# One decode step of grouped-query attention on one core: a tour of branches for TensorE, VectorE's heads as a loop, and the query loaded ahead of the first barriers

## The chip, the cores and the metric

The kernel runs on one core of a Trainium2 chip. The metric is the device time of one execution in microseconds, the median of three runs. The profile is that of one further execution, taken by the hardware profiler.

## The reference

One new token with 32 query heads attends to 65536 keys and values of 8 key/value heads, each of width 128, all in bfloat16. Each key/value head serves four query heads.

```python
B, Hq, Hkv, Sq, Sk, D = 1, 32, 8, 1, 65536, 128
scale = D ** -0.5
scores = jnp.einsum("bhqd,bhkd->bhqk", q, k) * scale   # k, v repeated for 4 query heads
p = _softmax(scores, axis=-1)
return jnp.einsum("bhqk,bhkd->bhqd", p, v)
```

K and V are 134 MB each. Each element is read once.

## The kernel before

The 8 key/value heads are taken one after the other (g = 0 to 7). The keys of a head lie in HBM as 128 partitions x 512 rows of 128 elements; one load (`load`, L116, issued by SyncE) brings half of them, 8 MB, as 128 rows of 64 KB. There are three buffers of that size: `bufA` and `bufB` take the two halves of K, `bufC` the two halves of V, one at a time. The last V goes elsewhere, as nothing more is to come: its first half to `bufA`, its second to `bufB` in seven pieces of `PIECES` rows, each with a semaphore of its own (`sP[0]` to `sP[6]`).

Each engine has its program written out by hand, with semaphores between them. The order of the loads is that of SyncE's queue (L132 to L155), each after the wait that says its buffer is free.

- VectorE (L199 to L258) first makes selector matrices out of an identity, and turns the query. Then, for each head, written out eight times: it turns each buffer of K in place, in two halves (`turn`, L221); takes the maximum of the scores (`mx`, L232); scales the result of the head before (`o_out`, L237); reduces the maxima further (`m4`, `mrow`, `nmb`); turns the exponentials (`E`, L254); takes the reciprocal of the sum (`rl`).
- TensorE (L298 to L438) makes the scores with `scores` (L316, 32 matmuls of 512 columns for each half buffer), the maxima with `maxima`, the sum with `sums`, and the product with V with `stream` (L333: four rows of V in one matmul of 512 columns, on one quarter of the array's columns, into `psum_o`). `pick` (L341) adds the diagonal blocks of `psum_o` by a selector into `psum_f`. Head 0's scores stand ahead of a loop of seven turns (L367), each with V of head g-1 and the scores of head g. Behind the loop comes the last V: `stream` on bufA; `idle(8)`, 16 matmuls whose results nobody reads; `stream` on the first piece; `idle(8)`; `stream` on the second piece; `pick`; then `quads` (L386, one row of V in a matmul of 128 columns, into `psum_s`) for the third and fourth pieces; `singles` (L395, straight into `psum_f`) for the last three; and one matmul (L433) that adds `s_sb`, the copy of `psum_s`.
- ScalarE copies `psum_o` to `o_sb`, makes the exponentials (L281), and at the end copies `psum_s` to `s_sb` (L289), scales the last head (L292) and stores it.
- GpSimd builds the constants, and for each head the stationary operand `wq` from the query (L183).

Ahead of all this stands the first load of `bufA`, issued between two barriers of all engines; everything else, the load of the query by ScalarE's queue (L261) too, is behind the second one.

Of the kernel before, what the change touches and what calls it, by code (L numbers as in the profile page):

```python
# [6 lines left out]

ALU = mybir.AluOpType
ACT = mybir.ActivationFunctionType
AX = mybir.AxisListType  # L10

G = 8
H = 4
P = 128
# [4 lines left out]
SLIDE = P + 4 * (W - 1)  # L19
PIECES = (128, 72, 28, 16, 4, 4, 4)  # L20


@with_exitstack
def kernel(
# [5 lines left out]
    out: bass.AP,  # L30
):


# [58 lines left out]
    kt = sem("kt")  # L92
    kdone = sem("kdone")
    vdone = sem("vdone")
# [4 lines left out]
    nms = sem("nms")  # L99
    qps = sem("qps")  # L100
    exd = sem("exd")
    ets = sem("ets")
    ocp = sem("ocp")
    outs = sem("outs")
    dl = sem("dl")
    pl = sem("pl")
    cleared = list(sems)
    sS = sem("sS")
# [13 lines left out]

    first = load(bufA, kr[0], 0)
    tc.no_tile_sem_insts.add(first.ins.name)
    first.then_inc(sA, 16)
    tc.add_to_no_dep_group("first", first.ins)
    tc.declare_fence(pool.nop().ins, group="first")
    tc.close()
    tc.compile()
# [4 lines left out]
    for g in range(1, G):  # L134
        sp.wait_ge(kdone, 2 * g - 1)
        load(bufA, kr[g], 0).then_inc(sA, 16)
        if g == 1:
            sp.wait_ge(kdone, 2)
            load(bufB, kr[1], 1).then_inc(sB, 16)
            sp.wait_ge(vdone, 1)  # L140
            load(bufC, vr[0], 1).then_inc(sC, 16)
            continue
        sp.wait_ge(vdone, 2 * (g - 1))
        load(bufC, vr[g - 1], 0).then_inc(sC, 16)
        sp.wait_ge(kdone, 2 * g)
        load(bufB, kr[g], 1).then_inc(sB, 16)
        sp.wait_ge(vdone, 2 * (g - 1) + 1)
        load(bufC, vr[g - 1], 1).then_inc(sC, 16)
    sp.wait_ge(kdone, 2 * G - 1)
    load(bufA, vr[G - 1], 0).then_inc(sA, 16)  # L150
    sp.wait_ge(kdone, 2 * G)
    at = 0
# [25 lines left out]
    for g in range(G):  # L178
        if g == 0:
            pool.wait_ge(exd, 1)  # L180
        else:
            pool.wait_ge(kdone, 2 * g)
        pool.tensor_tensor(  # L183
            out=wv[:, :, :, 0:H],
            in0=qv[:, :, g * H:(g + 1) * H].unsqueeze(2).broadcast_to([P, 4, 4, H]),
            in1=quad[:, :].unsqueeze(1).unsqueeze(3).broadcast_to([P, 4, 4, H]),
            op=ALU.mult,
        ).then_inc(wqs, 1)


    n_dl = [0]

    def after(ins):

        ins.then_inc(dl, 1)
        n_dl[0] += 1
        dve.wait_ge(dl, n_dl[0])

    dve.wait_ge(cst, 1)  # L199
    dve.tensor_reduce(  # L200
        out=quad[:, :], in_=ident[:, :].rearrange("p (a x) -> p a x", a=4), axis=AX.X, op=ALU.max
    )
    dve.tensor_reduce(
        out=selq[:, :], in_=ident[:, :].rearrange("p (j x) -> p x j", x=32), axis=AX.X, op=ALU.max
    )
    dve.tensor_reduce(
        out=sel[:, :], in_=ident[:, :].rearrange("p (x h) -> p h x", h=H), axis=AX.X, op=ALU.max
    )
    after(dve.tensor_reduce(
        out=s64[:, :], in_=ident[:, :].rearrange("p (j x) -> p x j", x=64), axis=AX.X, op=ALU.max  # L210
    ))
    dve.tensor_tensor(out=selx[:, :], in0=s64[:, 0:16], in1=s64[:, 48:64], op=ALU.add).then_inc(cst, 1)
# [9 lines left out]

    n_pes = 0
    for g in range(G):
        dve.wait_ge(sA, 16 * (g + 1))
        turn(bufA, 0)
        turn(bufA, 1)
        dve.wait_ge(sB, 16 * (g + 1))
        turn(bufB, 0)
        turn(bufB, 1)  # L230
        dve.wait_ge(kdone, 2 * (g + 1))
        dve.tensor_reduce(out=mx[:, :], in_=sc[:, :], axis=AX.X, op=ALU.max).then_inc(mxs, 1)  # L232
        if g > 0:

            n_pes += 1
            dve.wait_ge(pes, n_pes)
            dve.tensor_scalar_mul(  # L237
                out=o_out[:, (g - 1) * D:g * D], in0=psum_f[0:H, 0:D], scalar1=rl[:, 0:1]
            ).then_inc(outs, 1)
        n_pes += 1  # L240
        dve.wait_ge(pes, n_pes)
        after(dve.tensor_reduce(
            out=m4[:, :], in_=misc[0:1, 0:P].rearrange("o (x h) -> o h x", h=H), axis=AX.X, op=ALU.max
        ))
        dve.tensor_scalar_mul(
            out=mrow[:, :].rearrange("o (x h) -> o x h", h=H),
            in0=m4[:, :].unsqueeze(1).broadcast_to([1, 32, H]),
            scalar1=-SCALE,
        ).then_inc(mxs, 1)
        n_pes += 1  # L250
        dve.wait_ge(pes, n_pes)
        dve.tensor_copy(out=nmb[:, :], in_=misc[:, P:P + 1]).then_inc(nms, 1)  # L252
        dve.wait_ge(exd, g + 2)
        dve.transpose(out=E[:, 0:2048], in_=E[:, 0:2048]).then_inc(ets, 1)  # L254
        n_pes += 1
        dve.wait_ge(pes, n_pes)
        dve.reciprocal(out=rl[:, :], in_=misc[0:H, P + 4:P + 5]).then_inc(dl, 1)
        n_dl[0] += 1  # L258


    act.dma_start(out=qn[:, :], in_=q[0, :, 0, :]).then_inc(sQ, 16)  # L261
    act.wait_ge(qps, 1)
    act.copy(
        out=qx[:, :].rearrange("p (b r h) -> p b h r", b=2, r=2),
        in_=misc[:, 0:P].rearrange("p (b h r) -> p b h r", b=2, r=2),
    ).then_inc(exd, 1)

    def store(g, n):

        act.wait_ge(outs, g + n)  # L270
        act.dma_start(
            out=out[0, g * H:(g + n) * H, 0, :].rearrange("(g h) d -> h g d", h=H),
            in_=o_out[:, g * D:(g + n) * D].rearrange("h (g d) -> h g d", d=D),
        ).then_inc(sS, 16)

    for g in range(G):
# [7 lines left out]
        ).then_inc(exd, 1)  # L284
    store(0, G - 1)
    act.wait_ge(vdone, 2 * G)
    act.copy(out=o_sb[:, :], in_=psum_o[:, :]).then_inc(ocp, 1)  # L287
    act.wait_ge(vdone, 2 * G + 1)
    act.copy(out=s_sb[:, :], in_=psum_s[:, 0:D]).then_inc(ocp, 1)  # L289
    act.wait_ge(pes, n_pes + 1)  # L290
    act.wait_ge(dl, n_dl[0])
    act.activation(  # L292
        out=o_out[:, (G - 1) * D:G * D], in_=psum_f[0:H, 0:D], func=ACT.Copy, scale=rl[:, 0:1]
    ).then_inc(outs, 1)
    store(G - 1, 1)


    pe.wait_ge(cst, 4)  # L298
    pe.matmul(out=misc[:, 0:P], lhsT=rep[:, :], rhs=qt[:, :], start=True, stop=True).then_inc(qps, 1)  # L299

    def take(semaphore, n=1):

        pe.wait_ge(semaphore, n).then_inc(semaphore, -n)  # L303

    def scores(buf, x, s):

        take(kt)
        bank = sc[:, (2 * s + x) * 512:(2 * s + x + 1) * 512]
        T = buf[:, x * half // 2:(x + 1) * half // 2].rearrange(
            "p (c w b i r) -> p w b r c i", c=C, w=W, b=2, r=2  # L310
        )
        for w in range(W):
            for b in range(2):
                for r in range(2):
                    at = (2 * b + r) * SLIDE + 4 * (W - 1 - w)
                    last = pe.matmul(  # L316
                        out=bank, lhsT=wq[:, at:at + P], rhs=T[:, w, b, r],
                        start=(w + b + r == 0), stop=(w == W - 1 and b + r == 2),
                    )
        return last  # L320

# [4 lines left out]

    def stream(buf, s, lo, n, end):

        for row in range(lo, lo + n, 4):
            j = row // 4  # L330
            qd = slice(32 * (j % 4), 32 * (j % 4) + 32)
            at = column(s, row) // 32 * 32
            last = pe.matmul(  # L333
                out=psum_o[qd, :], lhsT=E[:, at:at + 32], rhs=buf[:, row * D:(row + 4) * D],
                start=(s == 0 and j < 4), stop=(s == 1 and row >= end - 16),
            )
        return last

# [8 lines left out]
    def maxima():  # L347
        take(mxs)
        pe.transpose(out=misc[0:1, 0:P], in_=mx[:, :], identity=ident[:, :]).then_inc(pes, 1)  # L349
        take(mxs)  # L350
        pe.matmul(  # L351
# [3 lines left out]
    def sums():  # L355
        take(ets)
        pe.matmul(  # L357
            out=misc[0:H, P + 4:P + 5], lhsT=sel[:, :], rhs=lsum[:, :], start=True, stop=True
        ).then_inc(pes, 1)

    take(wqs)
    scores(bufA, 0, 0)
    scores(bufA, 1, 0).then_inc(kdone, 1)
    scores(bufB, 0, 1)
    scores(bufB, 1, 1).then_inc(kdone, 1)
    maxima()
    with pe.Fori(1, G):  # L367
        sums()
        take(sC, 16)
        stream(bufC, 0, 0, NT, NT).then_inc(vdone, 1)  # L370
        take(wqs)
        scores(bufA, 0, 0)
        scores(bufA, 1, 0).then_inc(kdone, 1)
        scores(bufB, 0, 1)
        take(sC, 16)
        stream(bufC, 1, 0, NT, NT).then_inc(vdone, 1)
        scores(bufB, 1, 1).then_inc(kdone, 1)
        take(ocp)
        pick(True, True).then_inc(pes, 1)
        maxima()  # L380
# [28 lines left out]
    sums()  # L409
    pe.wait_ge(sA, 16 * (G + 1))  # L410
    stream(bufA, 0, 0, NT, NT).then_inc(vdone, 1)
    idle(8)
    at = 0
    for x in range(2):
        pe.wait_ge(sP[x], 16)
        last = stream(bufB, 1, at, PIECES[x], PIECES[0] + PIECES[1])
        at += PIECES[x]
        if x == 0:
            idle(8)
    last.then_inc(vdone, 1)  # L420
# [16 lines left out]
    pe.wait_ge(sP[6], 16)  # L437
    singles(at, PIECES[6], True).then_inc(pes, 1)  # L438

# [35 lines left out]
```

## Time and profile before

| | us |
|---|---|
| median of three runs (628.48 to 628.68) | 628.51 |
| the profiled execution | 628.52 |
| its span, first to last instruction | 626.6 |
| PE busy | 343.8 |
| DVE busy | 322.7 |
| ACT busy | 23.8 |
| POOL busy | 4.1 |
| HBM read | 268.44 MB |

In the views of the profile, PE is TensorE's matmuls, PEld its weight loads, DVE VectorE, ACT ScalarE, POOL GpSimd, SP SyncE. A row of the timeline gives the start, the duration, the engine, the line, the operation, the tiles written and read, the shape and the count; in brackets stands the engine's idle time before it and what ended it. A row of digits gives the busy share of equal slices in tenths. The program has two semaphore counts that matter below: `kdone`, which TensorE raises when it has used bufA and bufB of K, and for which SyncE, VectorE and GpSimd all wait; and `vdone`, the same for V.

### The profile page before, as it was taken

To read this page: it belongs to the slowest core of one execution; us is meant where nothing else is said; L and a number is where in the kernel's file an instruction comes from. 1 tells how busy PE (TensorE), PEld (TensorE's weight loads), DVE (VectorE), ACT (ScalarE), POOL (GpSimd) and SP (SyncE) were. 2 spreads that over 40 slices of the span, in tenths; PEclk is the share of its full clock that TensorE was granted. 3 is DMA by queue.
4 is the path that set the end of the run, shared out by engine and by line. 5 is a ranking of instruction groups with operands and counts; after the bars stand their busy time and mean duration, and the time that the engine had idled before them with its cause. 6 is when DMAs were issued, how large, how long until landed. Compare 5 with 4: busy or idle time off the path is not lost. (4 is left out here: it accounts for less than half of the span.)

```text
span 626.6 us, 4811 instructions
## 1 busy us (share of the span) xinstructions
PE 343.8 (55%) x2221; PEld 147.7 (24%) x2229; DVE 322.7 (52%) x93; ACT 23.8 (4%) x28; POOL 4.1 (1%) x19
## 2 busy tenths in 40 slices
PE   0097438850848408594094830948209592094957
PEld 0043213320323203231041310413104141041423
DVE  0587378539055490644906459073680826708230
ACT  1000100010000100001000010000100001000010
POOL 1000000000000000000000000000000000000000
PEclk9998679885798757787588975889658796597979
DMA  9999999999999999999999999999999999999997
GB/s 402 402 469 403 464 406 461 410 457 410 460 410 460 410 460 406 452 414 427 443 423 448 414 452 418 452 418 452 418 452 414 456 414 456 414 456 410 452 396 300
DMA packets 5565, 268.53 MB, mean 429 GB/s; under 512 B 696, under 2 KB 1080, under 8 KB 1336
## 3 DMA queue, kind: packets, MB, share of 16 engines
q1 hardware_dynamic: 5472, 268.44, 99.2%
q8 instruction: 4, 0.07, 0.0%
q10 hardware_dynamic: 88, 0.02, 0.0%
q14 instruction: 1, 0.01, 0.0%
HBM read 268.44 MB, written 0.01 MB: 428 GB/s over the span
## 5 line engine op out<-in xcount | busy, mean ns | idle before, releaser
L221 DVE STREAM_TRANSPOSE bufB<-bufB 128x8192 f32<-128x8192 f32 x16 | 138.4, 8690 | 130.5 <-DMA bufB<-in_k_dram 130.5
L316 PE MATMUL sc<-bufB,wq 128*128 128x512 bf16 x512 | 129.6, 415 | 55.8 <-PEq L303 55.8
L221 DVE STREAM_TRANSPOSE bufA<-bufA 128x8192 f32<-128x8192 f32 x16 | 138.2, 8673 | 15.5 <-DMA bufA<-in_k_dram 15.5
L333 PE MATMUL psum_o<-bufC,E 128*32 128x512 bf16 x896 | 66.2, 461 | 125.2 <-PEq L303 125.2
L316 PE MATMUL sc<-bufA,wq 128*128 128x512 bf16 x512 | 116.9, 387 | 27.7 <-PEq L303 27.7
L316 PEld LDWEIGHTS sc<-bufB,wq 128*128 128x128 bf16 x512 | 51.5, 103 | 133.4 <-issue 84.6
L316 PEld LDWEIGHTS sc<-bufA,wq 128*128 128x128 bf16 x512 | 49.2, 97 | 94.7 <-issue 37.1
L232 DVE TENSOR_REDUCE mx<-sc 128x1 f32<-128x2048 f32 x8 | 18.3, 2292 | 97.6 <-PE sc L316 97.6
L333 PEld LDWEIGHTS psum_o<-bufC,E 128*32 128x32 bf16 x896 | 29.8, 114 | 158.8 <-issue 146.8
L254 DVE STREAM_TRANSPOSE E<-E 128x2048 bf16<-128x2048 bf16 x8 | 18.5, 2312 | 17.0 <-ACT E L281 17.0
L357 PE MATMUL misc<-lsum,sel 128*4 128x1 f32 x16 | 1.5, 163 | 38.2 <-PEq L303 38.2
L279 ACT COPY o_sb<-psum_o 128x512 f32<-128x512 f32 x7 | 4.1, 585 | 437.1 <-PE psum_o L333 437.1
L281 ACT ACTIVATE E<-sc,nmb 128x2048 bf16<-128x2048 f32 x8 | 15.7, 1967 | 130.3 <-DVE nmb L252 130.3
L357 PEld LDWEIGHTS misc<-lsum,sel 128*4 128x4 f32 x16 | 0.9, 83 | 38.7 <-issue 38.7
L349 PE MATMUL misc<-ident,mx 128*1 128x128 f32 x8 | 2.3, 282 | 13.0 <-PEq L303 13.0
L341 PE MATMUL psum_f<-o_sb,selx 128*4 128x128 f32 x64 | 8.3, 273 | 0.7 <-ACT o_sb L287 0.7
L299 PE MATMUL misc<-qt,rep 32*128 32x128 bf16 x1 | 0.3, 284 | 13.2 <-DVE qt L214 13.2
L405 PE MATMUL sc<-bufA,wq 128*128 128x512 bf16 x24 | 6.7, 379 | 0.5 <-issue 0.2
L351 PE MATMUL misc<-one,mrow 1*128 1x1 f32 x16 | 3.4, 279 | 5.7 <-PEq L303 5.7
L341 PEld LDWEIGHTS psum_f<-o_sb,selx 128*4 128x4 f32 x64 | 4.9, 86 | 5.2 <-issue 3.0
L183 POOL TENSOR_TENSOR wq<-qx,quad 128x64 bf16<-128x64 bf16 x8 | 2.3, 292 | 512.9 <-PE sc L316 502.4
L333 PE MATMUL psum_o<-bufA,E 128*32 128x512 bf16 x64 | 5.3, 504 | 0.0
(41 smaller groups left out, 34.9 us busy)
## 6 DMA issues: line engine op xcount, KB each, us to landing
bufB<-in_v_dram SPq DMA_DIRECT2D x1, 4096.0 KB, 18.2
bufB<-in_v_dram SPq DMA_DIRECT2D x1, 2304.0 KB, 23.4
bufB<-in_v_dram SPq DMA_DIRECT2D x1, 896.0 KB, 25.1
bufB<-in_v_dram SPq DMA_DIRECT2D x1, 512.0 KB, 25.8
bufB<-in_v_dram SPq DMA_DIRECT2D x3, 128.0 KB, 25.5
bufC<-in_v_dram SPq DMA_DIRECT2D x14, 34.9
bufA<-in_k_dram SPq DMA_DIRECT2D x8, 37.4
bufB<-in_k_dram SPq DMA_DIRECT2D x8, 47.2
```

The lines of the kernel that those rows point to most:

```text
L183: pool.tensor_tensor(out=wv[:, :, :, 0:H], in0=qv[:, :, g * H:(g + 1) * H].unsqueeze(2).broadcast_to([P, 4, 4, H]), in1=quad[:, :].unsquee ...
L221: dve.transpose(out=kv, in_=kv).then_inc(kt, 1)
L232: dve.tensor_reduce(out=mx[:, :], in_=sc[:, :], axis=AX.X, op=ALU.max).then_inc(mxs, 1)
L254: dve.transpose(out=E[:, 0:2048], in_=E[:, 0:2048]).then_inc(ets, 1)
L279: act.copy(out=o_sb[:, :], in_=psum_o[:, :]).then_inc(ocp, 1)
L281: act.activation(out=E[:, 0:2048], in_=sc[:, :], func=ACT.Exp, bias=nmb[:, 0:1], scale=SCALE, accum_out=lsum[:, 0:1],).then_inc(exd, 1)
L316: last = pe.matmul(out=bank, lhsT=wq[:, at:at + P], rhs=T[:, w, b, r], start=(w + b + r == 0), stop=(w == W - 1 and b + r == 2),)
L333: last = pe.matmul(out=psum_o[qd, :], lhsT=E[:, at:at + 32], rhs=buf[:, row * D:(row + 4) * D], start=(s == 0 and j < 4), stop=(s == 1 and ...
L341: last = pe.matmul(out=psum_f[0:H, 0:D], lhsT=selx[:, H * x:H * x + H], rhs=o_sb[:, x * D:(x + 1) * D], start=(start and x == 0), stop=(st ...
L351: pe.matmul(out=misc[:, P:P + 1], lhsT=mrow[:, :], rhs=one[:, :], start=True, stop=True).then_inc(pes, 1)
L357: pe.matmul(out=misc[0:H, P + 4:P + 5], lhsT=sel[:, :], rhs=lsum[:, :], start=True, stop=True).then_inc(pes, 1)
L405: pe.matmul(out=sc[:, 0:512], lhsT=wq[:, 0:P], rhs=bufA[:, 0:512], start=True, stop=True)
```

## The change

Five things are changed.

1. **A tour.** TensorE gets three `stop`s in its program: at each, the work branches past one instruction, which branches to the next stop. The stops lie in the second half of the first head's scores, in the loop within the second `stream`, and behind the first piece of the last V. Ahead of the second barrier, TensorE branches to the first stop, from there to the second, the third, and back to `tour_end`. All engines are held at that barrier until it is there.
2. **VectorE's heads as a loop.** The eight written-out heads become a loop of eight turns with a branch for g = 0. For that, semaphores are no longer counted up but taken down at each wait (`take`), and split: `kdone` becomes `ka` (TensorE has used bufA), `scd` (TensorE has made all scores; VectorE takes it) and `kb` (VectorE passes it on, for the load of bufB and for `wq`). The column of `o_out` comes from the loop's register; the last head's result goes to column block 0, the others to the block one higher than before.
3. **The query's load** is issued by ScalarE's queue next to the first load of bufA, ahead of the barriers.
4. **The pieces** of the last half of V are 84 and 16 rows instead of 72 and 28, for the second and third of seven.
5. `exd`, `pes` and `dl` each lose some of their uses to semaphores of their own (`qxs`, `end`, `rls`).

```diff
-PIECES = (128, 72, 28, 16, 4, 4, 4)
+PIECES = (128, 84, 16, 16, 4, 4, 4)
...
-    first = load(bufA, kr[0], 0)
-    tc.no_tile_sem_insts.add(first.ins.name)
-    first.then_inc(sA, 16)
-    tc.add_to_no_dep_group("first", first.ins)
+    first = [
+        load(bufA, kr[0], 0).then_inc(sA, 16),
+        act.dma_start(out=qn[:, :], in_=q[0, :, 0, :]).then_inc(sQ, 16),
+    ]
+    for x in first:
+        tc.no_tile_sem_insts.add(x.ins.name)
+        tc.add_to_no_dep_group("first", x.ins)
     tc.declare_fence(pool.nop().ins, group="first")
+    stops = 3
+    home = nc.cur_bb.parent
+    with tc.tile_critical(sync_engine=mybir.EngineType.PE, no_gpsimd_drain=True):
+        going = pe.alloc_register("going")
+        pe.reg_mov(going, 1)
+        pe.br_lt(going, 2, on_true="stop_1", on_false="tour_end")
+        nc.switch_bb("tour_end", parent=home)
+        pe.nop().then_inc(tour, 1)
     tc.close()
...
-        sp.wait_ge(kdone, 2 * g - 1)
+        sp.wait_ge(ka, g)
         load(bufA, kr[g], 0).then_inc(sA, 16)
...
-        sp.wait_ge(kdone, 2 * g)
+        sp.wait_ge(kb, g)
         load(bufB, kr[g], 1).then_inc(sB, 16)
...
+    def take(engine, semaphore, n=1):
+        engine.wait_ge(semaphore, n).then_inc(semaphore, -n)
...
-    for g in range(G):
-        dve.wait_ge(sA, 16 * (g + 1))
+    with dve.Fori(0, G) as g:
+        take(dve, sA, 16)
         turn(bufA, 0)
         turn(bufA, 1)
...
-        dve.wait_ge(kdone, 2 * (g + 1))
+        take(dve, scd)
         dve.tensor_reduce(out=mx[:, :], in_=sc[:, :], axis=AX.X, op=ALU.max).then_inc(mxs, 1)
-        if g > 0:
-            n_pes += 1
-            dve.wait_ge(pes, n_pes)
+        dve.nop().then_inc(kb, 1)
+        with dve.If(g > 0):
+            take(dve, rls)
+            take(dve, pes)
             dve.tensor_scalar_mul(
-                out=o_out[:, (g - 1) * D:g * D], in0=psum_f[0:H, 0:D], scalar1=rl[:, 0:1]
+                out=o_out[:, ds(g * D, D)], in0=psum_f[0:H, 0:D], scalar1=rl[:, 0:1]
             ).then_inc(outs, 1)
...
-    act.dma_start(out=qn[:, :], in_=q[0, :, 0, :]).then_inc(sQ, 16)
...
+    def stop(x):
+        pe.br(f"past_{x}")
+        with nc.body(f"stop_{x}", parent=home, valid_engines=[pe.engine]):
+            pe.nop()
+            pe.br(f"stop_{x + 1}" if x < stops else "tour_end")
+        nc.switch_bb(f"past_{x}")
...
-    scores(bufB, 0, 1)
-    scores(bufB, 1, 1).then_inc(kdone, 1)
+    scores(bufB, 0, 1, 6)
+    scores(bufB, 1, 1).then_inc(scd, 1)
...
-        stream(bufC, 1, 0, NT, NT).then_inc(vdone, 1)
+        stream(bufC, 1, 0, NT, NT, 172).then_inc(vdone, 1)
...
         if x == 0:
+            stop(3)
             idle(8)
```

The fourth argument of `scores` and the last of `stream` say after which step the stop stands.

## The prediction

> **What bounds the kernel now.** I read the page first, for the share of each engine and of the DMA.
>
> ```profile
> span 626.6 us, 4811 instructions
> ...
> PE 343.8 (55%) x2221; PEld 147.7 (24%) x2229; DVE 322.7 (52%) x93; ACT 23.8 (4%) x28; POOL 4.1 (1%) x19
> ...
> DMA  9999999999999999999999999999999999999997
> ...
> q1 hardware_dynamic: 5472, 268.44, 99.2%
> q8 instruction: 4, 0.07, 0.0%
> ...
> q14 instruction: 1, 0.01, 0.0%
> ```
>
> No compute engine is busy for much over half the span, and the DMA is full from first slice to last. Following the DMA records packet by packet, the 16 DMA engines run without a gap: a 64 KB row takes 2.418 us, the first one starts at 1.74 us, and no engine pauses for over 0.1 us in sum before its last packet. The time is therefore: start of the first packet, plus the work of the slowest DMA engine, plus a tail behind the last landing. An edit counts only if it moves one of these three.
>
> The slowest DMA engine is the second view: the DMA of 620.5 to 624.5, 40 slices of 0.1 us.
>
> ```profile
> DMA  9989996999999999844132333332221000000000
> ```
>
> All engines work until about 622.2; then a few go on to 623.9. At the end of the last 8 MB load the records give twelve engines within 0.42 us of each other, and four behind the first of them by 1.12, 1.46, 1.57 and 1.92 us. Each of the four took its step back at one packet: 16 KB on q8 at 55.8, 94.7 and 125.8 us (steps of 1.45 to 1.53 us, packets of 0.94 to 1.08 us) and 8 KB on q14 at 261.4 us (1.0 us). The fourth q8 packet, at 612.0, sets back a fifth engine that was early. These are fetches of program code: counted in the program's listing, the four on q8 lie some 256 TensorE instructions apart. As every load is split evenly over the 16 engines, an engine once behind stays behind: the slowest costs about 1.5 us, 1.92 against the undisturbed 0.42.
>
> Third, the end of the timeline, where the tail is.
>
> ```profile
> 619.97 1.26 PE L333 MATMUL psum_o<-bufB,E 128*32 128x512 bf16 x18
> ...
> 621.26 0.59 ACT L287 COPY o_sb<-psum_o 128x512 f32<-128x512 f32 x1 [19.01 <-PE psum_o L333]
> ...
> 621.90 0.82 PE L341 MATMUL psum_f<-o_sb,selx 128*4 128x128 f32 x6 [0.68 <-ACT o_sb L287]
> ...
> 623.40 0.23 PEld L386 LDWEIGHTS psum_s<-bufB,E 128*32 128x32 bf16 x16 [0.25 <-DMA bufB<-in_v_dram]
> ...
> 623.86 0.27 ACT L289 COPY s_sb<-psum_s 128x128 f32<-128x128 f32 x1 [2.01 <-PE psum_s L386]
> ...
> 624.40 0.61 PE L395 MATMUL psum_f<-bufB,E 128*4 128x128 bf16 x8
> 625.05 0.36 ACT L292 ACTIVATE o_out<-psum_f,rl 4x128 bf16<-4x128 f32 x1 [0.92 <-PE psum_f L395]
> ```
>
> The piece of 72 rows is usable at 619.97; `stream`, the copy to `o_sb` and `pick` follow, and the first 28 `quads` start their last matmul at 623.11. The 16 rows of `sP[3]` arrive at 623.40: the PE chain that begins with the second piece has 0.29 us to spare there. From 623.40 on it is a straight line to the end.
>
> The sum is made on the profiled execution: 628.52 us, of which 626.6 are the span and 1.9 lie around it. It is 0.01 from the median of 628.51. The three runs span 0.2 us; 0.2% (1.26 us) is about what a measurement of this kernel can tell from no change.
>
> **The pieces, 72/28 to 84/16.** The same bytes land at the same end, but the second piece is 12 rows later: 28 rows took 2.185 us on the slowest engine (from 619.416 to 621.601), so 12 take 0.93 and the piece is usable at 620.90. `stream` runs 21 matmuls for 18, which is 5.25 groups of four at 0.216 us for 4.5: about 0.2 more, since a new group is begun. `o_sb` is then written to 622.99 and the last pass of `pick` starts at 623.80 (622.67 before). All 32 `quads` follow without waiting; eight groups at 0.056 us and a matmul of 0.22 end near 624.5, against 623.81. **+0.7 us**, on the path, as the 0.29 to spare are used up. With a faster clock or no wait at all the bound from below is 0.93 + 0.2 - 0.29 - 0.17 (the 12 quads fewer ahead of `sP[3]`), that is 0.67, less what the last 16 gain by following at once, some 0.2: +0.5. From above +0.9.
>
> **The tour.** It removes no fetch: the same pages past the first two must come once, now at the start. In the trace of before, page 2 is fetched as TensorE enters page 1. The tour begins after the first barrier (PE's sequencer is through it at 0.72 us; the move and the branches cost some 0.1 to 0.2 each, as the idle loop's compare-and-branch of 0.21 shows), so the first fetch is asked for at about 1.2 us, close to the load's first packet at 1.74. The others come while bufA loads. What a fetch costs its DMA engine is 1.45 us by the rows above. If they hit random engines, the slowest is some 0.27 (the mean of the later of two bases between 0 and 0.42) plus 1.45: 1.72 for 1.92. **-0.2 us**; between -0.5 (a fetch on the earliest engines alone) and 0 (the same engines as now). Should a fetch have held TensorE up in the body, nothing was lost by it: every load is issued 10 us or more ahead of its first packet, the last one 6.
>
> The wait that the tour adds: all engines stand at the second barrier until TensorE is home. Behind it on SP are the loads of bufB and bufC (now issued at 1.89 and 2.27), on POOL the constants, behind these DVE's `select` and the query chain, which now ends at 14.7 us with the write of `wq`. bufA occupies the DMA until 21.83, and a packet starts 1.0 us after its issue (0.74 to 1.74), so SP may issue as late as 20.8. The query's packets show how long a small packet waits in this stage: issued at 1.91, ready near 2.9, run at 7.31, behind two packets that were already begun. A fetch then takes up to 4.84 + 1.0 us. With three waits in a row the tour ends between 9 us (the first one free) and 19 us (1.2 + 3 x 5.84); with 0.6 for the barrier, SP issues at 10 to 19.6. Cost: nothing, hidden by the first load; DVE needs its first K at 22.6. The Trainium skill, "DMA: Bandwidth & Descriptors", Queues, rings and completion order, says that an engine drains a whole packet of typically 9 to 17 descriptors from one queue before it turns to the next; by that rule a fetch could stand behind all eight rows of bufA on its engine, until 21.8 us, and rival (b) would hold. The query, which got in after two rows, disagrees with it.
>
> In the body each stop costs two branches of about 0.1 to 0.2 us on TensorE's sequencer, which runs ahead of the matmuls; the third lies ahead of `idle`, whose end now has 0.3 us to the second piece and will have 0.9 more. Nothing.
>
> **DVE as a loop.** Per head some ten `take`s of 0.02 to 0.05 us (the semaphore instructions at the start of the trace show that) and three branches. The branch on g is taken while the 2.29 us reduce still runs. In the last head E may be ready 0.2 to 0.8 us later; `stream` on bufA and `idle` end at 613.63 and wait until 614.46 for the first piece, so 0.83 hide it. The `kb` signal follows the taking of `scd` by about 0.1, or by 2.4 if it waits for the reduce. It releases the bufB loads and POOL's `wq`; the last bufB loads are issued at 596.19 and their first packet is due at 602.28: 5.1 to spare after the 1.0 of latency. Every other load has 10 or more. Nothing. The fetch on q14 goes with the unrolled code, but its engine (1.12) is not the slowest.
>
> **The query ahead of the barriers.** 32 packets of 0.018 us, two on each engine, now perhaps ahead of bufA: 0 to +0.1 us, I take 0.05. It also lands before anyone can use it; the wait of 9.0 us of DVE for `qn` goes, and the wait for the tour takes its place.
>
> Sum: 628.52 + 0.7 - 0.2 + 0.05 = 629.07, say **629.0**.
>
> **Rivals.** (a) The fetches cost no DMA engine anything, because they run ahead of or inside the slow start of the load (its first 16 packets take 3.05 to 3.39 us where 2.42 is usual, so 0.6 to 0.9 may be free). Then the slowest engine is 1.5 us earlier: 628.52 - 1.5 + 0.7 = 627.7, 627.5 with the pieces at their lower bound, and 627.0 if they are free besides. For it speaks the first fetch, against it the later ones, at 5 us and after, where the records show full steps. (b) Slower: the tour outlasts the first load. It decides from an SP issue at 20.8 us; each us past that stops all DMA engines for one. With four waits of 5.84 from 1.2, the tour ends at 24.6 and SP issues at 25.2: +4.4, so 633.5 with the pieces. Against it: page 0 is where the tour starts, and three waits are enough by the listing. (c) The change doesn't do what it says: pages fetched by the tour are not there when the work comes, and are fetched again. Then a slowest engine has two steps, 0.42 + 2.9 for 1.92: +1.4, with the pieces 630.6. Two tour pages on one DMA engine cost the same. The rows speak against losing pages: TensorE's loop jumps back some 550 instructions six times, and not one packet of q8 lies between 125.8 and 612.0. The Trainium skill, "Runtime: NRT & Kernel Launch", Instruction fetch mechanics, says that the store holds only two 16 KiB lines and that a taken branch out of them forces a fetch before execution can go on; by that rule the tour would be thrown away, and rival (c) holds. The trace, with no fetch in those six jumps, disagrees.
>
> **How the numbers follow.** My forecast, 628.5 to 629.7: 0.66. Rival (a), 627.0 to 628.3: 0.13. Rival (c) with the shared engine, 629.9 to 631: 0.13. Rival (b), above 631: 0.08. The range 627.6 to 630.6 leaves out most of (b) and the edges of (a) and (c), some 0.18. Faster by over 0.2% (below 627.25) is only the far edge of (a): 0.05. Slower by over 0.2% (above 629.77) is (b), (c) and a little of the forecast's upper edge: 0.24. The rest, 0.71, is the same.
>
> **What would show it.** Right: q8 packets in the first 20 us and none later; bufB's first load issued between 8 and 20 us; DMA engines without gaps; some engines about 1.7 us behind at the end; `pick` starting near 622.9 with no wait for DMA between the two `quads`. Wrong: a hole in the DMA row near 22 us (b); q8 packets in the body (c); all engines ending within 0.5 us (a); `quads` still waiting for `sP[3]`, which would make the pieces free.

## The result, and the profile after

| | us |
|---|---|
| before, median of 7 runs (628.45 to 628.68) | 628.51 |
| changed, median of 7 runs (630.47 to 630.84) | 630.71 |
| ratio changed / before | 1.0034 (1.0022 to 1.0046) |
| span of the profiled execution, before and after | 626.6, 628.9 |

The changed kernel is slower by 2.2 us, 0.34%. The prediction said 629.0, no change that can be told; the time lies just above its range. The page of the changed kernel, the rows that stood for before:

```profile
span 628.9 us, 4951 instructions
...
PE 344.9 (55%) x2220; PEld 148.0 (24%) x2220; DVE 323.2 (51%) x93; ACT 23.8 (4%) x28; POOL 4.1 (1%) x19
...
DMA  9999999999999999999999999999999999999996
...
q1 hardware_dynamic: 5472, 268.44, 98.9%
q8 instruction: 4, 0.07, 0.1%
```

The bytes and the number of TensorE's code fetches are the same, the busy times nearly so; q14's fetch is gone. The same four q8 packets took 5.59 us in sum, 4.03 before (the page rounds their share to 0.1% and 0.0%): that is the trace of the cause. The DMA records give the fetches at 7.60, 7.64, 16.91 and 21.98 us, with 1.79, 2.04, 0.88 and 0.88 us. This is the window of 7 to 10 us (a packet counts whole in the window in which it starts, so a share can exceed 100%):

```profile
q1 hardware_dynamic: 27, 1.77, 140.5%
q8 instruction: 2, 0.03, 8.0%
```

Two pages run at once, and a 64 KB row behind each of them takes 3.43 and 3.56 us instead of 2.42, so they lie on two DMA engines. In the kernel before, a window of the same length around one fetch, 54 to 57 us, has a quarter of that share:

```profile
q8 instruction: 1, 0.02, 2.1%
```

There a q8 fetch took 0.94 to 1.08 us and the row behind it 2.89 to 2.97.

The end, DMA of 621.9 to 625.9 in slices of 0.1 us (the window shown of before was 620.5 to 624.5, 1.4 earlier):

```profile
DMA  9999999976534333021011010111111110000000
```

Most engines stop by 623, several 0.7 us later than in the kernel before; a thin trail, from 623.6 on mostly of two engines, goes on to 625.4. The tail of the timeline:

```profile
622.39 1.47 PE L355 MATMUL psum_o<-bufB,E 128*32 128x512 bf16 x21 [0.94 <-DMA bufB<-in_v_dram]
...
623.89 0.58 ACT L303 COPY o_sb<-psum_o 128x512 f32<-128x512 f32 x1 [19.65 <-PE psum_o L355]
...
624.53 0.82 PE L365 MATMUL psum_f<-o_sb,selx 128*4 128x128 f32 x6 [0.67 <-ACT o_sb L303]
...
625.30 0.71 PE L410 MATMUL psum_s<-bufB,E 128*32 128x128 bf16 x26
...
626.61 0.61 PE L419 MATMUL psum_f<-bufB,E 128*4 128x128 bf16 x8
...
627.32 0.36 ACT L308 ACTIVATE o_out<-psum_f,rl 4x128 bf16<-4x128 f32 x1 [0.98 <-PE psum_f L419]
```

The last wait for DMA is now that of the second piece, at 622.39; from there on no row waits for a load, and both groups of `quads` run in one go.

Two numbers split the difference exactly. The last packet of a load ends at 625.44, before at 623.90: +1.53. From there to the end of the span it is 3.45, before 2.71: +0.74. The sum is the 2.27 by which the span grew. The same two numbers from the profile of each kernel below (these profiles are single executions, so a few tenths may differ from the medians):

| kernel | last 8 MB load ends on its slowest engine | last packet | from there to the end | median us |
|---|---|---|---|---|
| before | 604.21 | 623.90 | 2.71 | 628.51 |
| changed | 605.77 | 625.44 | 3.45 | 630.71 |
| e1, old pieces | 606.06 | 625.73 | 2.73 | 630.46 |
| e2, no tour | 604.06 | 623.75 | 3.47 | 629.22 |
| e3, loads ahead of the tour | 605.75 | 625.42 | 3.46 | 630.75 |
| e4, before with 84 and 16 | 604.08 | 623.77 | 3.38 | 629.12 |
| e5, one stop | 604.11 | 623.81 | 3.43 | 629.19 |
| e6, two stops | 605.65 | 625.30 | 3.49 | 630.66 |
| e7, four stops | 604.08 | 623.78 | 3.45 | 629.12 |
| e8, loads behind the tour | 613.59 | 633.31 | 3.41 | 638.64 |
| e9, two stops, 72 and 28 | 606.10 | 625.77 | 3.08 | 630.04 |
| e10, four stops, 72 and 28 | 603.85 | 623.54 | 2.81 | 628.39 |
| e11, loop and query, 72 and 28 | 604.15 | 623.83 | 3.34 | 628.85 |

### The profile page after: what moved, and what is told of

Read it like the earlier page. It is cut to its first block, busy times and chain, and to the rows that moved or that the text cites. A ratio compares the mean times of both kernels' runs of the same rounds, so it can differ in the third digit from the quotient of the medians.

```text
span 628.9 us, 4951 instructions
## 1 busy us (share of the span) xinstructions
PE 344.9 (55%) x2220; PEld 148.0 (24%) x2220; DVE 323.2 (51%) x93; ACT 23.8 (4%) x28; POOL 4.1 (1%) x19
## 5 line engine op out<-in xcount | busy, mean ns | idle before, releaser
L336 PE MATMUL sc<-bufA,wq 128*128 128x512 bf16 x512 | 118.1, 391 | 18.6 <-PEq L215 18.6
L429 PE MATMUL sc<-bufA,wq 128*128 128x512 bf16 x32 | 7.3, 380 | 0.0
```

What stands on the lines that cost most here:

```text
L336: last = pe.matmul(out=bank, lhsT=wq[:, at:at + P], rhs=T[:, w, b, r], start=(w + b + r == 0), stop=(w == W - 1 and b + r == 2),)
L429: pe.matmul(out=sc[:, 0:512], lhsT=wq[:, 0:P], rhs=bufA[:, 0:512], start=True, stop=True)
```

## The experiments

The kernel before ran beside each: 628.39 (23 runs) beside e1 to e4, 628.41 (21 runs) beside e5 to e8, 628.47 (27 runs) beside e9 to e11.

My theory after the result (A) had three terms: the pieces, an empty DMA queue at 22 us, and fetches of double price. Rivals were VectorE's loop (B) and the two set-back engines alone (C).

**e1: the old pieces in the changed kernel.**

```diff
-PIECES = (128, 84, 16, 16, 4, 4, 4)
+PIECES = (128, 72, 28, 16, 4, 4, 4)
```

> The changed kernel with the pieces of before (72 and 28 rows). Theory A says that the 2.2 us are three terms: the pieces (0.7), an empty DMA queue at 22 us (0.7: SyncE issued the second load at 20.79, and the twelve least disturbed DMA engines are 0.7 later than before from then on) and the two code fetches at 7.6 us that set their DMA engines back by 3.0 us each where 1.5 was usual (0.8). A: 630.0. Rival B, the pieces cost nothing and VectorE's loop delays the end: 630.7.

Measured: 630.46 us (629.75 to 630.88), ratio 1.0032 (1.0020 to 1.0043). Inconclusive: it lies between the two, with runs spread over 1.1 us where the changed kernel's lie within 0.4. In the profiled execution the tail is back at 2.73 us, but the last packet ends at 625.73, 0.3 later than in the changed kernel; the rows behind its two early fetches take 3.79 and 3.50 us. e9 and e11 take this up.

**e2: no tour.**

```diff
-    with tc.tile_critical(sync_engine=mybir.EngineType.PE, no_gpsimd_drain=True):
...
-        nc.switch_bb("tour_end", parent=home)
-        pe.nop().then_inc(tour, 1)
...
     def stop(x):
+        pass
```

> The changed kernel without tour and stops; the loop on VectorE, the early query and the pieces of 84 and 16 stay. Theory A: the code fetches go back into the body, no hole in the DMA at 22 us; only the pieces are left, 628.5 + 0.7 = 629.2. Rival B (VectorE's loop delays the end): 630.0 or more.

Measured: 629.22 us (629.03 to 629.36), 1.0012 (1.0003 to 1.0021). As A said. The tour costs 1.5 us, loop and query nothing beside the pieces of 84 and 16.

**e3: the first loads of bufB and bufC ahead of the tour.**

```diff
         act.dma_start(out=qn[:, :], in_=q[0, :, 0, :]).then_inc(sQ, 16),
+        load(bufB, kr[0], 1).then_inc(sB, 16),
+        load(bufC, vr[0], 0).then_inc(sC, 16),
     ]
```

> The changed kernel with the first loads of bufB and bufC issued next to that of bufA, ahead of the barrier that holds everything until the tour is over. Theory A: the DMA queue never runs empty, 630.7 - 0.7 = 630.0; the two set-back DMA engines keep their lag. Rival C (the set-back engines alone decide, as they never ran empty): 630.7, or more, since in the changed kernel they made up some of their lag while the others started anew.

Measured: 630.75 us (630.54 to 630.85), 1.0036 (1.0022 to 1.0049). A falls in this term, C holds. In the changed kernel SyncE issued late:

```profile
20.79 0.33 SPq L125 DMA_DIRECT2D bufB<-in_k_dram  x1
```

Its first rows come at 21.87 and later and take up to 3.13 us (at the start of the program up to 3.41); in e3 the same rows take 2.42. This set most engines back by some 0.7 us, but not the two slow ones, which were still busy with bufA until 25.07 and 25.23. In e3 the early engines end the last 8 MB load at 602.2 instead of 602.95, the slowest at 605.75 instead of 605.77. The hole is real, and costs nothing because it falls on engines that have time.

**e4: the new pieces in the kernel before.**

```diff
-PIECES = (128, 72, 28, 16, 4, 4, 4)
+PIECES = (128, 84, 16, 16, 4, 4, 4)
```

> The kernel before with the pieces of 84 and 16 alone. Theory A: 628.5 + 0.7 = 629.2, with the fourth piece no longer waited for. Rival, the pieces are free: 628.5.

Measured: 629.12 us (628.89 to 629.30), 1.0010 (1.0001 to 1.0019). The pieces alone cost 0.73.

So 1.5 us hang on the two early fetches. New theory (D): a page fetched alone sets its DMA engine back by 1.45 us, and two fetched together set theirs back by 3.0 each. Rival (E): any fetch in the first load is that dear.

**e5 and e6: one stop, two stops.** The second and third stop are left out (e5, the edit shown), or the third alone (e6, `stops = 2`); the rest is the changed kernel.

```diff
-    stops = 3
+    stops = 1
...
     def stop(x):
+        if x > stops:
+            return
```

> The changed kernel with the first stop alone: the tour enters page 1, which asks for page 2, and goes home without waiting. Theory D: the slowest DMA engine decides, and it is slow because two pages were fetched at the same time (own packets of 1.8 and 2.0 us and next rows of 3.4 and 3.6, a step of 3.0 us each), while one page alone costs a step of 1.45. D: one page early with a step of 1.45, the others in the body as in the kernel without tour: 629.2. Rival E: any fetch within the first load costs 3.0, since that load is just starting: 630.7.

> The changed kernel with the first two stops: pages 2 and 3 are asked for within half a microsecond, the tour is home near 12 us, and SyncE issues long before the first load ends. Theory D: the two engines are set back by 3.0 us each and decide: 630.7, though the DMA never runs empty and the third stop is gone. If the third stop or the hole at 22 us mattered: 629.2 to 630.0.

Measured: e5 629.19 us (629.08 to 629.35), 1.0012 (1.0003 to 1.0021); e6 630.66 us (630.53 to 630.80), 1.0035 (1.0021 to 1.0049). The DMA of 7 to 10 us, first e5, then e6:

```profile
q8 instruction: 1, 0.02, 2.0%
```

```profile
q8 instruction: 2, 0.03, 7.6%
```

One page, at 7.29 us, in the middle of the first load: 0.96 us, the row behind it 2.87, and the engine is 1.05 us behind the next slowest at the end of that load, 1.55 behind the earliest. Two pages: 1.53 and 2.11 us, rows of 3.56 and 3.16. E falls. In e6 the tour is home near 12 us, there is no hole and no third stop, and all of the loss is there.

TensorE's branches show why the two pages come together. In e5 the branch home from the first stop lasts 0.18 us and the tour is home at 1.90 us, while the fetch runs only at 7.29: the first stop sets off a fetch and nothing waits for it. In the changed kernel the branch from the first stop to the second lasts 9.98 us, with two fetches under way.

**e7: four stops.** A stop in page 2 as well, in the loop, within the scores of bufA's second half, and the loads of e3; the two stops behind it become the third and the fourth.

```diff
-    stops = 3
+    stops = 4
...
-        scores(bufA, 1, 0).then_inc(ka, 1)
+        scores(bufA, 1, 0, 2, 2).then_inc(ka, 1)
...
```

> The changed kernel with a stop in page 2 as well, so that each page is entered from the one before it and is fetched alone; bufB and bufC are loaded ahead of the tour, which will last some 25 to 30 us. Theory D: four steps of 1.45, slowest engine as in the kernel without tour: 629.2, if the late start of VectorE (up to 8 us) is caught up. Rival E: 630.7.

Measured: 629.12 us (628.95 to 629.28), 1.0010 (1.0001 to 1.0019). The fetches come at 7.59, 14.90, 21.89 and 29.10 us, each alone, with 0.89 to 0.96 us and rows of 2.86 to 2.97 behind them. Loss gone: the last packet is back at 623.78. This is the DMA of 620.5 to 624.5, with the trail of the kernel before and not that of the changed one:

```profile
DMA  9999878999999999861231222222211100000000
```

From e3, which has the same loads ahead of the tour and lost 1.6 us more, e7 differs by the one stop alone. TensorE is home at 24.5 us, later than in the changed kernel, and that costs nothing.

**e8: all loads behind the tour.**

```diff
-    first = [
-        load(bufA, kr[0], 0).then_inc(sA, 16),
-        act.dma_start(out=qn[:, :], in_=q[0, :, 0, :]).then_inc(sQ, 16),
-    ]
...
+    load(bufA, kr[0], 0).then_inc(sA, 16)
     load(bufB, kr[0], 1).then_inc(sB, 16)
```

> The changed kernel with all loads behind the tour, so that the pages are fetched while the DMA has nothing else to do. Theory D: no DMA engine is set back, all end within 0.5 us; the first row starts some 7 us later than now (a guess from three waits of 2 us); 630.7 + 7 - 2.4 = 635.3. Rival: the set-back is no matter of fetches, and the engines are spread as before: 637.7.

Measured: 638.64 us (638.52 to 638.81), 1.0162 (1.0147 to 1.0178). By its time alone the rival's 637.7 is nearer than the 635.3 of theory D, since the first row starts at 12.61 us and not near 9: even with the DMA idle the tour takes until 10.4. The spread decides, and it speaks for D: the first row starts 10.88 us later than in the changed kernel, the last packet ends only 7.87 us later, so the 3.0 us are given back. DMA of 629.9 to 633.9:

```profile
DMA  9999999999999899999889999999996420000000
```

All engines stop together; 0.76 us lie between first and last at the end of the last 8 MB load, where the kernel before has 1.92 and the changed one 2.82. The two pages fetched at once took 1.68 and 2.00 us with nothing else on the DMA, the two single ones 1.28 and 1.39.

**e9, e10, e11: the old pieces again.** The one-line edit of e1 in e6 (e9), in e7 (e10) and in e2 (e11).

> Two stops as before, now with the pieces of 72 and 28. With the whole tour the old pieces gave back only 0.25 us; there the hole at 22 us and a fourth fetch added their own scatter. If the pieces cost 0.7 on top of the set-back: 630.7 - 0.7 = 629.9. If the late engines hide most of the pieces' cost, or TensorE's own chain (stream on bufA, idle, first piece, idle) has become the bound: 630.4.

> Four stops, pages fetched one at a time, bufB and bufC loaded ahead of the tour, pieces of 72 and 28. Theory D: nothing is left of the 2.2 us, 628.4, the time of the kernel before: the tour gives nothing and costs nothing, as each page still sets its engine back by 1.45 us. A gain would need 628.2 or less.

> VectorE's loop and the early query alone: no tour, pieces of 72 and 28. Theory D: 628.4 to 628.5, the same as the kernel before; the fetch for VectorE at 261 us goes, but its engine was never the slowest. If loop or query cost something that the other edits hid: 628.7 or more.

Measured: e9 630.04 us (629.80 to 630.87), 1.0025 (1.0016 to 1.0034). e10 628.39 us (628.22 to 629.10), 1.0001 (0.9992 to 1.0010). e11 628.85 us (628.50 to 629.22), 1.0005 (0.9996 to 1.0014).

e9 is 0.62 under e6: the pieces cost about their full price beside the set-back too. e10 is the kernel before again; nothing of the change is left in the time but also nothing gained. e11 lies 0.4 above its expectation. Its interval includes no change, but 628.85 is on the side that the expectation gave to a hidden cost, and 6 of its 11 runs are slower than the slowest of the 27 of the kernel before. Its profiled execution has the whole loss in the tail: 3.34 us, 2.71 before. The runs of e1, e9, e10 and e11 spread over 0.7 to 1.1 us; the kernel before, which has the old pieces too but no loop, spreads over 0.6 to 0.8. The timeline of e11's profile (629.07) names what can be late there; the first row is that of the kernel before, the others are e11's:

```profile
604.80 5.27 PE L333 MATMUL psum_o<-bufA,E 128*32 128x512 bf16 x61
```

```profile
605.28 6.53 PE L342 MATMUL psum_o<-bufA,E 128*32 128x512 bf16 x61
...
615.30 1.91 PE L342 MATMUL psum_o<-bufB,E 128*32 128x512 bf16 x32
...
620.70 1.26 PE L342 MATMUL psum_o<-bufB,E 128*32 128x512 bf16 x18
```

None of e11's three waits for DMA. `stream` on bufA took 6.5 us, in the kernel before 5.27: the granted clock was 0.60 in 608 to 612 us, against 0.98 before. As the head's end is also 0.4 later with the loop, TensorE reaches the second piece at 620.70, 0.7 after it could have been used (619.97 before). With 84 and 16 the second piece lands near 620.7 anyway, so this lateness is covered, and those kernels' runs lie within 0.4 us. That it explains every high run of e1, e9 and e10 was not shown: of the four, e9 (6.27) and e11 (6.53) have the long `stream` in their profiles, e1 (5.51) and e10 (5.32) do not. The other profiles lie between 5.27 and 6.21.

No variant beat the kernel before, and none of these runs points to one that would: each still has at least one fetch at full price while the DMA is loaded, or pays for an idle DMA with 10 us.

## Why the prediction was wrong

- **The step that failed is the tour's term**, "What a fetch costs its DMA engine is 1.45 us by the rows above", and from it **-0.2 us**. The price was right for one page at a time (e5, e7) and too small for two together: 3.0 us each. The term is +1.5 us: the slowest engine ends the last 8 MB load at 605.77 for 604.21. Even with single fetches the gain of 0.2 did not show: the slowest engine ends at 604.08 in e7, at 604.06 without a tour (e2). All four rows that I took the price from were of fetches 30 us or more apart, and I counted three waits in a row without asking whether the first stop already sets off a fetch that the jump to the second does not wait for. The trace of before could not show two at once; the bound from above should have allowed for it. The 0.42 us within which I put the undisturbed engines are 0.31 by the records, which moves the term by 0.1 at most.
- **Rival (c)** had nearly the time, 630.6, through two tour pages on one DMA engine. They were on two engines, running at the same time, and slowed each other. Its main part, pages lost and fetched again, did not happen: e7 has its four fetches by 30 us and none in the body. So the two lines that I took from the Trainium skill, "Runtime: NRT & Kernel Launch", Instruction fetch mechanics, do not describe TensorE; I had passed over that the same section gives PE a store of 128 KiB, where most engines have 32. The trace agrees with the larger one: in e7 four pages of 16 KB are fetched by 30 us, and no q8 packet follows through eight heads.
- **Rival (b)**, the empty queue: the tour ended at 19.65 us, just above my 9 to 19, and SyncE issued at 20.79, at the point I gave (20.8). That my times came so near was luck: I had counted three waits of up to 5.84 us, and there were two, of 9.98 and 7.59. The hole came but cost nothing (e3): I had not thought of engines that are still busy with the first load.
- **Rival (a)**, free fetches, holds only with an idle DMA (e8), at a price of 10 us.
- **The pieces, +0.7**: right, 0.73 alone (e4) and 0.74 in the tail of the changed kernel, by the path I gave: the second piece, `stream`, `o_sb`, `pick`, then `quads` without a wait.
- **The loop, nothing**: right with these pieces (e2 against e4: 629.22 and 629.12). The stretch from the last `mx` to `stream` on bufA grew from 8.56 to 9.01 us, within my 0.2 to 0.8, and the cover I named, 0.83 before the first piece, went from 0.83 to 0.20. `kb` came 0.13 us after `scd` was taken. With the old pieces the cover can fail, and did in e11's profile, where the clock came late; I had not priced that.
- **The query, 0.05**: no cost seen; its packets ran from 4.73 us on, and the first row began at 1.73 as before.

## What to carry to other kernels

In this kernel, where all DMA engines are busy without a gap and every load is split evenly over them, the end was set by the slowest one, and what once delayed it stayed in the time until the end. In a kernel of this kind, look at the last slices of the DMA row for a thin trail, and search the records backwards for the packet that began it. Moving the disturbances to an earlier time did not remove them (e7), and moving two of them close together made them dearer (e6). A price read from events that came singly is a price for single events; when a change bunches them, its upper bound must come from elsewhere, or be left open.

## What the runs showed of the hardware

Two code fetches of 16 KB that overlapped took 1.5 to 2.1 us each, on different DMA engines and even with nothing else on the DMA (e8), against 0.9 to 1.4 for one alone. What they share was not tried; it is not the DMA engine.

The first 64 KB rows of a load that was issued only 1.1 us before the engines were free for it took 2.5 to 3.1 us (changed kernel, 21.87 to 22.85 us), where the same rows took 2.42 in e3, whose load had stood in the queue since 1.16 us. At the program's start the first rows took 2.6 to 3.4.
